# Attention pairs ahead of soft MoE slots: the V products of a pair moved into one block, one pair later

## Chip, cores, metric

The kernel runs on one core of one Trainium2 chip. The metric is the device time of one execution in microseconds (us). Smaller is better.

## The reference, cut to what matters

```python
# attention: q, k, v of 8 batches x 12 heads x 448 tokens x 64
scores = q @ k.T / 8
m = scores.max(-1)
e = exp(scores - m)
attn = e / (e.sum(-1) + exp(-m) + 1e-9)
x = attn @ v                       # then heads side by side: 3584 x 768
# soft MoE: phi 768 x 32, 8 experts of 4 slots, F = 1024
logits = x @ phi
d = softmax of logits over all tokens (per slot)
slot_input = d.T @ x
slot_out[e] = relu(slot_input[e] @ w1[e]) @ w2[e]
c = softmax of logits over the slots (per token)
out = c @ slot_out
```

## The kernel before

Two heads make a pair, and there are 48 pairs (`NPAIR`), six to a batch (`PB`) and three to a group (`NP`). One core does them one after the other; the order on every engine is the order in which the Python code emits the instructions (`manual_schedule`), so the loop over `s` at L646 is the schedule, written out by hand.

What is done to pair `n`:

- `T(n)` (L236): TensorE turns q and k, 28 transposes in quarter tiles (64x64) of the array, into one PSUM tile `ps_t`. From pair 8 on it comes from the pool `psA`, which has three buffers. VectorE (L257), or for every third pair ScalarE (L255), copies it to a tile of `qk_t`, of which there are `NQK` = 7.
- `A1(n, i, hl)` (L287) and `A(n, 3)` (L278): scores with queries on the partitions, each in a tile `ps_a` of the same pool `psA`; VectorE takes the row maxima from it (L292, L285). That makes seven `ps_a` and one `ps_t` for a pair, all through the three buffers in turn.
- `W2(g)`, `W3(g)` (L295, L305): for a group, the maxima are turned to a row by TensorE, three chunks in the full array (L299) and the half chunk in two quarter tiles (L302), and ScalarE copies them and takes the exponentials of the maxima.
- `Bk(n, 3)` (L318) and, inside `AB`, `scores` and `less` (L357, L361): scores with keys on the partitions, less the maxima, in tiles `ps_b` of the pool `psB` (four buffers); ScalarE takes the exponentials (L364, L343) into tiles `e2_t` (`NE` = 5, two heads in each) and `e1_t`.
- `AB(s, i)` (L347) puts six matmuls of half the array's rows together: one `A1` of a pair further ahead, two `scores`, two `less`, and the other `A1`. Two matmuls in different halves of the rows run at once.
- `AV(n, i, qs)` (L385): products of the exponentials with V, added up in the one tile `ps_av` of `psV`. For `qs` = `range(3)` each is in the full array; for `qs` = `[3]` it is in half the array's columns (128x64). 24 of the first kind and 8 of the second make a pair.
- `N1(n)` (L403) copies the result out of PSUM on ScalarE, `N2(n)` (L412) divides: two small VectorE instructions (L418, L419) and three on GpSimd (L423 to L428). `PX(n)` (L442) turns the result on TensorE, and ScalarE copies it (L455).
- `P(b)` (L462) is the soft MoE part of batch `b`, in six steps that the dictionary `post` (L590) lays into the pairs of the next batch.

A pair's round has two halves (`y`). In the first stand `AB(s,0)`, `AB(s,1)`, the V products `AV(s-1, 2..3)`, the eight half column ones of pair `s-1`, and `N1(s-1)`. In the second stand `AB(s,2)`, `Bk(s,3)`, `T(s+6)`, `W2`/`W3` in every third round, `AV(s, 0..1)`, a step of `post`, `PX(s-2)` and `N2(s-1)`. GpSimd's queue also issues the loads (`load`, `load_half`, `narrow`, L702 to L727) and places V (`V`, L376).

After the pairs, the expert matmuls (`hidden`, `turn`, `slots`) and the output follow; they depend on the last batch's maxima, and the output's writes end the kernel.

Of the kernel before, what the change touches and what calls it, by code (L numbers as in the profile page):

```python
# [24 lines left out]
HG = 6  # L25
NP = 3
W65 = 65
VS = 66


@with_exitstack
def kernel(
# [10 lines left out]
    nc = tc.nc  # L43
# [32 lines left out]

    NQK, NE, VPN, NATV = 7, 5, HG * 4 * VS, HG * 4 * D
    sizes = [("nq0", 2 * NP * S), ("nq1", 2 * NP * S), ("nv", NATV), ("qk6", 2 * S), ("wm1", 512),  # L80
             ("qk0", 2 * S), ("qk1", 2 * S), ("qk2", 2 * S), ("wm0", 512), ("qk3", 2 * S), ("vp0", VPN),
             ("qk4", 2 * S), ("x0", 4 * DD), ("qk5", 2 * S), ("e2", NE * 2 * S), ("e1", S), ("vp1", VPN),
             ("xT", KC * 512), ("x1", 4 * DD)]
# [5 lines left out]
    part = lambda nm, o, z: R[:, at_[nm] + o:at_[nm] + o + z]  # L89
    qk_t = [part(f"qk{i}", 0, 2 * S).rearrange("p (a s) -> p a s", a=2) for i in range(NQK)]  # L90
    e2_t = [part("e2", i * 2 * S, 2 * S).rearrange("p (h s) -> p h s", h=2) for i in range(NE)]
    e1_t = part("e1", 0, S)
    vp = [part(f"vp{i}", 0, VPN).rearrange("p (h i d) -> p h i d", h=HG, i=4) for i in range(2)]
    wm = [part(f"wm{i}", 0, 512).rearrange("p (i c) -> p i c", i=4) for i in range(2)]
    xb = [part(f"x{i}", 0, 4 * DD).rearrange("p (i d) -> p i d", i=4) for i in range(2)]
# [47 lines left out]
    with ExitStack() as at:  # L143
# [81 lines left out]

        ec, mT, eT, av, us = {}, {}, {}, {}, {}
        qkT = {}
        st = {"e2": 0}


        def kcol(hl, tok):
# [30 lines left out]
        mg = lambda n: 0 if n == 0 else n // NP + 1  # L262

        def top(n, i, hl=0):
            c = 64 * hl + n % NP
            return wm[mg(n) % 2][:, i, c:c + 1]

        def A(n, i):
            t = qkT[n]
# [25 lines left out]
        def W2(g):  # L295
            w = wm[g % 2]
            ps = pb_("ps_m")
            for i in range(3):
                nc.tensor.matmul(ps[:, i * 128:(i + 1) * 128], w[:, i, :], ident, start=True, stop=True)  # L299
            for hl in range(2):  # L300
                r = slice(64 - 64 * hl, 128 - 64 * hl)
                nc.tensor.matmul(ps[64 * hl:64 * hl + 64, 384:448], w[r, 3, 0:64], ident[r, r], start=True, stop=True)  # L302
            st["ps_m"] = ps

        def W3(g):  # L305
            t = psm.tile([128, S], BF16, tag="mT", name="mT")
            nc.scalar.copy(t, st["ps_m"][:, 0:S])
            mT[g] = t
            e = psm.tile([128, NP, 7], F32, tag="ec", name="ec", bufs=3)
            w = wm[g % 2]  # L310
            nc.scalar.activation(e[:, :, 0:6].rearrange("p l (i h) -> p i l h", i=3),
                                 w[:, 0:3, :].rearrange("p i (h c) -> p i c h", h=2)[:, :, 0:NP, :],
                                 AF.Exp, scale=-scale)
            nc.scalar.activation(e[:, :, 6], w[:, 3, 0:NP], AF.Exp, scale=-scale)
            ec[g] = e


        def Bk(n, i, c=0):  # L318

            g, pl = divmod(n, NP)  # L320
            t = qkT[n]
            rs = [slice(0, 64), slice(64, 128)]
            if i < 3:
                pss = [pb_("ps_b") for _ in range(2)]
                outs = [p[:, 0:S] for p in pss]
                cols = slice(i * 128, (i + 1) * 128)
                e = e2_t[st["e2"] % NE]
                st["e2"] += 1
                es = [e[:, hl, :] for hl in range(2)]
            else:  # L330
                pss = [pb_("ps_b")]
                outs = [pss[0][r, 0:S] for r in rs]
                cols = slice(384, 448)
                es = [e1_t]
            m = cols.stop - cols.start
            for hl in range(2):
                nc.tensor.matmul(outs[hl], t[rs[hl], 1, cols], t[rs[hl], 0, :], start=True, stop=False)  # L337
            As(c)
            for hl in range(2):
                nc.tensor.matmul(outs[hl], sel[rs[hl], pl:pl + 1].to_broadcast([64, m]), mT[mg(n)][rs[hl], :],  # L340
                                 start=False, stop=True)
            for p, e in zip(pss, es):
                nc.scalar.activation(e, p[:, 0:S], AF.Exp, scale=scale)  # L343
            for hl in range(2):
                eT[n, i, hl] = es[hl % len(es)]

        def AB(n, i):  # L347


            t, pl = qkT[n], n % NP  # L350
            run = runs.pop(0) if runs else None
            cols = slice(i * 128, (i + 1) * 128)
            e = e2_t[st["e2"] % NE]
            st["e2"] += 1
            rs, ps = [slice(0, 64), slice(64, 128)], {}

            def scores(hl):  # L357
                ps[hl] = pb_("ps_b")
                nc.tensor.matmul(ps[hl][:, 0:S], t[rs[hl], 1, cols], t[rs[hl], 0, :], start=True, stop=False)  # L359

            def less(hl):  # L361
                nc.tensor.matmul(ps[hl][:, 0:S], sel[rs[hl], pl:pl + 1].to_broadcast([64, 128]), mT[mg(n)][rs[hl], :],  # L362
                                 start=False, stop=True)
                nc.scalar.activation(e[:, hl, :], ps[hl][:, 0:S], AF.Exp, scale=scale)  # L364
                eT[n, i, hl] = e[:, hl, :]

            if run:
                A1(*run, 0)
            scores(1)
            scores(0)  # L370
            less(1)
            less(0)
            if run:
                A1(*run, 1)
# [87 lines left out]
        def P(b):  # L462
# [62 lines left out]

            def corr():
                if b:
                    t = psm.tile([128, NS], F32, tag="corr", name="corr")
                    nc.scalar.activation(t, v["z"][:, 8, :], AF.Exp)
                    v["corr"] = t  # L530

# [14 lines left out]
            def c_turn():  # L546
                ps = pa([128, 128], BF16, "ps_ct")
                nc.tensor.transpose(ps, flat(v["cd"][:, 0:4, :]), ident)
                nc.vector.tensor_copy(cT[:, b // 2, :, b % 2, :], ps.rearrange("p (h j) -> p h j", h=2))
                r = crec[:, b, :]  # L550
                nc.vector.reduce_sum(r, v["cd"][:, 0:4, :], axis=AX.X)
                nc.vector.tensor_scalar(r, r, 1e-9, None, op0=ALU.add)
                nc.vector.reciprocal(r, r)

            def s_add():
                if b:
# [4 lines left out]
            def s_last():  # L561

                h = KC // 2
                s_mm(0, h)
                nc.vector.tensor_add(siT[:, 0:h, :], acc[:, 0:h, :], v["ps_s"])
                s_mm(h, KC + 1)
                ps = v["ps_s"]
                nc.vector.tensor_add(siT[:, h:KC, :], acc[:, h:KC, :], ps[:, 0:KC - h, :])
                t = psm.tile([128, NS], F32, tag="corr", name="srow")
                nc.vector.scalar_tensor_tensor(t, acc[:, KC, :], 1e-9, ps[:, KC - h, :], op0=ALU.add, op1=ALU.add)  # L570

                nc.vector.tensor_mul(t, t, fold)
                nc.vector.reduce_sum(hrec, t, axis=AX.X)
                nc.vector.reciprocal(hrec, hrec)
# [12 lines left out]

        post = {}  # L590
        for b in range(B - 1):
            for z, f in enumerate(P(b)):
                post[2 * (PB * b + PB + 2) + z + (z > 2) + (z > 4) if b < B - 2 else 2 * (PB * b + PB + 2) - 1 + z] = f

        ub = ubuf.rearrange("p n c -> p (n c)").bitcast(BF16)
        take = lambda z, n: ub[:, z:z + n]
# [38 lines left out]
        for z in range(2):  # L635
# [4 lines left out]
        half_at = {s: i for i, s in enumerate((1, 4, 7, 10, 13, 16, 22, 25, 28, 31, 34))}  # L640

        narrow_at = {18: 4, 19: 5, 20: 6, 35: 7}
        part_at = {38: ((11, 0, 3),), 41: ((11, 3, 7),), 42: ((11, 7, 8),)}
        col_at = {42: ((0, 0, 8),), 43: ((1, 0, 2),), 44: ((1, 2, 6),), 45: ((1, 6, 8), (2, 0, 4), (3, 0, 6)),
                  46: ((2, 4, 8),), 47: ((3, 6, 8),)}
        for s in range(NPAIR):  # L646
            for y in range(2):
                hs = 2 * s + y
                early, last_ = int(hs < 5), int(hs < 3)
                if early:  # L650
# [13 lines left out]
                if hs < 5:  # L664
                    T(hs + 3)
                if y == 0:
                    if 0 <= s - 1:
                        for i in (2, 3):
                            AV(s - 1, i, range(3))
                else:  # L670
                    if 2 <= s < NPAIR - 6:
                        T(s + 6)
                    g = (s + 1) // 3
                    if (s + 1) % 3 == 0 and g < NG:
                        W2(g + 1)
                        W3(g + 1)
                    if s < NPAIR:
# [6 lines left out]
                if y and 0 <= s - 2 < NPAIR - 2 and s - 2 != n6:  # L684
                    PX(s - 2)
                if hs == 2 * n6 + 4:
                    PX(n6)
# [11 lines left out]
                if hs == 1:  # L699
                    W2(1)  # L700
                    W3(1)
            g = (s + 10) // 3  # L702
            if s == 1 or s % 3 == 2:
                g = 3 if s == 1 else g
                if (s == 1 or g > 3) and g < NG:
                    load(g, "q")
                    load(g, "k")
            g = (s + 9) // 3
            if s % 3 == 0 and g - 2 < NG:
                V(g - 2)  # L710
# [185 lines left out]
```

## Time and profile before

| what | value |
|---|---|
| runs | 307.33, 308.73, 309.12 us; median 308.73 us |
| profiled execution | 309.52 us, its span (first to last instruction) 307.7 us |
| busy in the span | TensorE 279.3 us (91%), VectorE 257.1 (84%), ScalarE 250.9 (82%), GpSimd 184.9 (60%) |
| chain that ended last | TensorE 69%, VectorE 14%, ScalarE 8%, issue 3% |
| granted TensorE clock | 1.00 up to 275 us, 0.58 in the last 32.7 us |
| pairs in their regular order | about 40 us to 240 us, 30.1 to 31.3 us for six pairs |
| maxima, L292 | 254 instructions, 140.0 us busy, 615 ns each |
| exponentials, L364 | 272 instructions, 131.0 us busy, 573 ns each |
| V products, L397 | 1536 instructions, 64.6 us busy |

Busy times are sums over the rows of an engine, with overlap counted once. A row of TensorE lasts from the start of a matmul until its last result is out (353 ns for 448 columns), though the next one begins much earlier; how fast TensorE goes is read from start to start. Rows of VectorE and ScalarE overlap a little too: a maximum has a row of 615 ns, but a run of six lasts less than six times that.

### The profile page before, as it was taken

Reading aid. Unit: us, or ns where it says so; the run is one execution under the profiler, and the core shown is the slowest. Engines: PE = TensorE matmul, PEld = TensorE weight load, DVE = VectorE, ACT = ScalarE, POOL = GpSimd, SP = SyncE. Lnnn points to the kernel's source line nnn. Section 1 sums busy time; section 2 is a strip of 40 time slices with the busy share of each in tenths; the row PEclk is TensorE's granted clock in tenths of the full one; section 3 lists DMA queues with packets and bytes.
Section 4 is the critical chain, followed back from the end, with each engine's and each line's share of the span. In section 5 each row is a group of like instructions: output and inputs, shape, how many; then the busy total and the mean of one; then the engine's idle time right before and its main releaser. Section 6 shows DMA issues by size and latency. Waiting matters only on the chain.

```text
span 307.7 us, 12173 instructions
## 1 busy us (share of the span) xinstructions
PE 279.3 (91%) x5097; PEld 159.8 (52%) x5097; DVE 257.1 (84%) x604; ACT 250.9 (82%) x551; POOL 184.9 (60%) x336
## 2 busy tenths in 40 slices
PE   7999999999999999999999999999999999995900
PEld 2444656566565656555656565656564555441100
DVE  7899999999999999989999999999999676446910
ACT  3477999999999999989999999999999995345800
POOL 9681986968586869866877677686747662000000
PEclk9999999999999999999999999999999999997555
DMA  8999999999999999999999999999845899909995
GB/s 134 134 158 184 139 210 202 195 197 165 191 161 198 164 200 148 202 184 151 120 202 134 197 179 204 151 200 205 141 56 88 124 137 224 362 32 341 433 426 229
DMA packets 49384, 57.69 MB, mean 188 GB/s; under 512 B 2865, under 2 KB 41521, under 8 KB 48945
## 3 DMA queue, kind: packets, MB, share of 16 engines
q0 software_dynamic: 45280, 42.29, 89.6%
q1 hardware_dynamic: 4048, 14.62, 12.1%
q8 instruction: 40, 0.66, 0.8%
q14 instruction: 16, 0.12, 0.1%
HBM read 88.18 MB, written 14.16 MB: 333 GB/s over the span
## 4 chain that ended last, share of the span: by engine, by line
PE 69%; DVE 14%; ACT 8%; issue 3%; POOL 1%; DVEq 0%; POOLq 0%
PE ps_av L397 15%; PE ps_a L291 9%; PE ps_t L251 7%; PE ps_b L359 7%; PE ps_b L362 6%; DVE R L292 6%; PE ps_b L337 4%; PE ps_b L340 2%; ACT R L343 2%; DVE R L277 2%; PE ps_x L449 2%; PE ps_o L802 2%; PE ps_a L274 2%; PE ps_so L773 2%; ACT R L255 2%
## 5 line engine op out<-in xcount | busy, mean ns | idle before, releaser
L292 DVE TENSOR_REDUCE R<-ps_a 128x1 bf16<-128x448 f32 x254 | 140.0, 615 | 6.4 <-PE ps_a L291 5.5
L364 ACT ACTIVATE R<-ps_b 128x448 bf16<-128x448 f32 x272 | 131.0, 573 | 0.5 <-PE ps_b L362 0.2
L291 PE MATMUL ps_a<-R 64*128 64x448 bf16 x254 | 83.2, 353 | 1.5 <-DVE R L292 1.5
L359 PE MATMUL ps_b<-R 64*128 64x448 bf16 x272 | 74.5, 353 | 1.1
L362 PE MATMUL ps_b<-mT,sel 64*128 64x448 bf16 x272 | 71.3, 350 | 0.0
L423 POOL TENSOR_TENSOR R<-ubuf,rec 128x384 bf16<-128x384 f32 x44 | 36.2, 823 | 55.1 <-DVE rec L419 33.7
L397 PEld LDWEIGHTS <-R 128*128 128x128 bf16 (+1 forms) x1536 | 50.0, 100 | 30.8 <-issue 26.1
L397 PE MATMUL ps_av<-R 128*128 128x65 bf16 (+1 forms) x1536 | 64.6, 196 | 0.0
L343 ACT ACTIVATE R<-ps_b 128x448 bf16<-128x448 f32 x64 | 35.9, 579 | 2.7 <-PE ps_b L340 2.6
L251 PEld LDWEIGHTS <-R 64*64 64x64 bf16 x1344 | 30.0, 112 | 12.6 <-issue 4.9
L455 ACT CAST R<-ps_x 128x512 bf16<-128x512 f32 x47 | 28.1, 599 | 6.9 <-PE ps_x L449 6.4
L251 PE MATMUL ps_t<-ident,R 64*64 64x64 bf16 x1344 | 31.2, 196 | 0.6
L285 DVE TENSOR_REDUCE R<-ps_a 128x1 bf16<-128x448 f32 x48 | 29.6, 617 | 0.6 <-PE ps_a L283 0.6
L362 PEld LDWEIGHTS <-sel 64*128 64x128 bf16 x272 | 21.8, 94 | 15.1 <-issue 5.5
L291 PEld LDWEIGHTS <-R 64*128 64x128 bf16 x254 | 23.8, 94 | 11.1 <-issue 1.1
L409 ACT COPY ubuf<-ps_av 128x455 f32<-128x455 f32 x44 | 25.1, 570 | 2.4 <-POOL R L428 2.2
L255 ACT COPY R<-ps_t 128x896 bf16<-128x896 bf16 x20 | 18.4, 922 | 6.0 <-PE ps_t L251 5.6
L337 PE MATMUL ps_b<-R 64*64 64x448 bf16 (+1 forms) x112 | 21.9, 375 | 0.0
L277 DVE TENSOR_REDUCE R<-ps_a 128x1 bf16<-128x448 f32 x34 | 18.9, 618 | 2.1 <-PE ps_a L274 2.0
L340 PE MATMUL ps_b<-mT,sel 64*64 64x448 bf16 (+1 forms) x112 | 20.5, 353 | 0.0
L428 POOL TENSOR_TENSOR R<-ubuf,rec 128x128 bf16<-128x128 f32 x44 | 17.5, 398 | 3.7
L359 PEld LDWEIGHTS <-R 64*128 64x128 bf16 x272 | 17.2, 94 | 4.7 <-issue 0.3
(137 smaller groups left out, 439.7 us busy)
## 6 DMA issues: line engine op xcount, KB each, us to landing
W<-in_moe_w_dram POOLq DMA_DIRECT2D x22, 768.0 KB, 10.2
R<-in_v_dram POOLq DMA_DIRECT2D x32, 192.0 KB, 4.9
out_dram<-W SPq DMA_DIRECT2D x2, 2688.0 KB, 11.8
R<-in_q_dram POOLq DMA_DIRECT2D x14, 336.0 KB, 7.9
R<-in_k_dram POOLq DMA_DIRECT2D x14, 336.0 KB, 9.0
wd<-in_moe_w_dram POOLq DMA_DIRECT2D x8, 384.0 KB, 10.7
R<-wd SPq DMA_DIRECT2D x8, 384.0 KB, 8.2
R<-in_moe_w_dram POOLq DMA_DIRECT2D x2, 768.0 KB, 8.1
```

The source lines that it names most:

```text
L251: nc.tensor.transpose(ps[r, a, c:c + 64], src[r, pl, tok * D:(tok + 1) * D], ident[r, r])
L285: nc.vector.reduce_max(top(n, i), ps[:, 0:S], axis=AX.X)
L291: nc.tensor.matmul(ps[:, 0:S], t[r, 0, i * 128:(i + 1) * 128], t[r, 1, :], start=True, stop=True)
L292: nc.vector.reduce_max(top(n, i, hl), ps[:, 0:S], axis=AX.X)
L337: nc.tensor.matmul(outs[hl], t[rs[hl], 1, cols], t[rs[hl], 0, :], start=True, stop=False)
L343: nc.scalar.activation(e, p[:, 0:S], AF.Exp, scale=scale)
L359: nc.tensor.matmul(ps[hl][:, 0:S], t[rs[hl], 1, cols], t[rs[hl], 0, :], start=True, stop=False)
L362: nc.tensor.matmul(ps[hl][:, 0:S], sel[rs[hl], pl:pl + 1].to_broadcast([64, 128]), mT[mg(n)][rs[hl], :], start=False, stop=True)
L364: nc.scalar.activation(e[:, hl, :], ps[hl][:, 0:S], AF.Exp, scale=scale)
L397: nc.tensor.matmul(o, eT[n, i, hl][:, qc], vp[g % 2][:, 2 * pl + hl, i, 0:W65], start=(i == 0 and u == 0 and hl == 0), stop=(i == 3), skip ...
L423: eng.tensor_mul(x[:, 0:3, c:c + 128].rearrange("p i (h d) -> p i h d", h=2), u[:, 0:6, 0:D].rearrange("p (i h) d -> p i h d", h=2), rec[: ...
L455: nc.scalar.copy(xT[:, pb, :], pss[0])
```

## The change

- From pair 3 (`S0`) to pair 40 (`S1` - 1) a round is written by a new function `pair(s)`. The three `AB` stand one after the other, then `Bk(s,3)`, `T(s+5)`, in every third round `W2`/`W3`, a step of `post`, `PX(s-3)`, and then all 32 V products of pair `s-1` in one block. `N1(s-1)` stands at the end, and `N2(s-2)` between the second and the third `AB`. The first three pairs and the last seven keep the old order, with a round in which it goes over at each end.
- For this there are six tiles of exponentials for two heads (`NE` and one more, `e5`), two for the half chunk (`e1_t`), and six tiles of turned q and k in place of seven. `T` runs five pairs ahead and not six.
- The half chunk's maxima lie elsewhere in `wm`, so that `W2` turns them by two matmuls over 128 and 120 columns in the full array's shape, not by two of 64x64.
- The steps of `post` go one to a round; `1e-9` and the reciprocal of `crec` are done once for all batches at the end, not per batch; the tile `corr` has one buffer.
- The loads of q and k stand at the end of rounds 0, 3, 6, ... and not 2, 5, 8, ...; the parts of one expert's weights (`part_at`) are loaded at 39 and 42, and not at 38, 41 and 42.

```diff
+HALF = 392
...
-    NQK, NE, VPN, NATV = 7, 5, HG * 4 * VS, HG * 4 * D
+    NQK, NE, VPN, NATV = 6, 5, HG * 4 * VS, HG * 4 * D
...
-    e1_t = part("e1", 0, S)
+    e2_t.append(part("e5", 0, 2 * S).rearrange("p (h s) -> p h s", h=2))
+    e1_t = [part("e1", 0, S), keep.tile([128, S], BF16, name="e1b")]
...
+        def next_e2(n):
+            if n == S1 and NE in free:
+                free.remove(NE)
+            free.append(free.pop(0))
+            return e2_t[free[-1]]
...
-            for hl in range(2):
-                r = slice(64 - 64 * hl, 128 - 64 * hl)
-                nc.tensor.matmul(ps[64 * hl:64 * hl + 64, 384:448], w[r, 3, 0:64], ident[r, r], start=True, stop=True)
+            f = w.rearrange("p i c -> p (i c)")
+            nc.tensor.matmul(ps[:, 384:448], f[:, HALF - 64:HALF + 64], ident[:, 0:64], start=True, stop=False)
+            nc.tensor.matmul(ps[0:512 - HALF, 384:448], f[:, HALF:512], ident[:, 64:128], start=False, stop=True)
...
-                nc.vector.reduce_sum(r, v["cd"][:, 0:4, :], axis=AX.X)
-                nc.vector.tensor_scalar(r, r, 1e-9, None, op0=ALU.add)
-                nc.vector.reciprocal(r, r)
+                nc.vector.reduce_sum(crec[:, b, :], v["cd"][:, 0:4, :], axis=AX.X)
+                if b == B - 1:
+                    nc.vector.tensor_scalar(crec, crec, 1e-9, None, op0=ALU.add)
+                    nc.vector.reciprocal(crec, crec)
...
+        S0, S1 = 3, NPAIR - 7
...
-                post[2 * (PB * b + PB + 2) + z + (z > 2) + (z > 4) if b < B - 2 else 2 * (PB * b + PB + 2) - 1 + z] = f
+                if b == B - 2:
+                    post[2 * (PB * b + PB + 2) - 1 + z] = f
+                elif PB * b + PB + 3 + z < S1:
+                    post[2 * (PB * b + PB + 3 + z) + 1] = f
+                else:
+                    post[max(post) + 1] = f
...
-        part_at = {38: ((11, 0, 3),), 41: ((11, 3, 7),), 42: ((11, 7, 8),)}
+        part_at = {39: ((11, 0, 3),), 42: ((11, 3, 8),)}
...
+        def pair(s):
+            AB(s, 0)
+            AB(s, 1)
+            if s > S0:
+                N2(s - 2)
+            AB(s, 2)
+            Bk(s, 3, 1)
+            T(s + 5)
+            if (s + 1) % 3 == 0:
+                W2((s + 1) // 3 + 1)
+                W3((s + 1) // 3 + 1)
+            if 2 * s + 1 in post:
+                post[2 * s + 1]()
+            PX(s - 3)
+            for i in range(4):
+                AV(s - 1, i, range(3))
+            for i in range(4):
+                AV(s - 1, i, [3])
+            N1(s - 1)
+
         for s in range(NPAIR):
-            for y in range(2):
+            if S0 <= s < S1:
+                pair(s)
+            for y in range(0 if S0 <= s < S1 else 2):
...
-            g = (s + 10) // 3
-            if s == 1 or s % 3 == 2:
-                g = 3 if s == 1 else g
-                if (s == 1 or g > 3) and g < NG:
-                    load(g, "q")
-                    load(g, "k")
+            g = 3 if s == 1 else (s + 9) // 3
+            if (s == 1 or s > 2 and s % 3 == 0) and g < NG:
+                load(g, "q")
+                load(g, "k")
```

More of the change, by code (lines that the diff above doesn't have):

```diff
@@ L75 @@
     halfm = const.tile([128, 2], F32, name="halfm")
-    NQK, NE, VPN, NATV = 7, 5, HG * 4 * VS, HG * 4 * D
-    sizes = [("nq0", 2 * NP * S), ("nq1", 2 * NP * S), ("nv", NATV), ("qk6", 2 * S), ("wm1", 512),
+    NQK, NE, VPN, NATV = 6, 5, HG * 4 * VS, HG * 4 * D
+    sizes = [("nq0", 2 * NP * S), ("nq1", 2 * NP * S), ("nv", NATV), ("e5", 2 * S), ("wm1", 512),
              ("qk0", 2 * S), ("qk1", 2 * S), ("qk2", 2 * S), ("wm0", 512), ("qk3", 2 * S), ("vp0", VPN),
@@ L227 @@
         qkT = {}
-        st = {"e2": 0}
+        st = {"e1": 0}
+        free = list(range(NE + 1))
+        def next_e2(n):
[3 more added lines that the diff above has]
+            return e2_t[free[-1]]
         def kcol(hl, tok):
@@ L264, in top @@
         def top(n, i, hl=0):
-            c = 64 * hl + n % NP
-            return wm[mg(n) % 2][:, i, c:c + 1]
+            c = n % NP + (HALF if i == 3 else i * 128 + 64 * hl)
+            return wm[mg(n) % 2].rearrange("p i c -> p (i c)")[:, c:c + 1]
         def A(n, i):
@@ L313, in W3 @@
                                  AF.Exp, scale=-scale)
-            nc.scalar.activation(e[:, :, 6], w[:, 3, 0:NP], AF.Exp, scale=-scale)
+            nc.scalar.activation(e[:, :, 6], w[:, 3, HALF - 384:HALF - 384 + NP], AF.Exp, scale=-scale)
             ec[g] = e
@@ L326, in Bk @@
                 cols = slice(i * 128, (i + 1) * 128)
-                e = e2_t[st["e2"] % NE]
-                st["e2"] += 1
+                e = next_e2(n)
                 es = [e[:, hl, :] for hl in range(2)]
@@ L333, in Bk @@
                 cols = slice(384, 448)
-                es = [e1_t]
+                es = [e1_t[st["e1"] % 2]]
+                st["e1"] += 1
             m = cols.stop - cols.start
@@ L352, in AB @@
             cols = slice(i * 128, (i + 1) * 128)
-            e = e2_t[st["e2"] % NE]
-            st["e2"] += 1
+            e = next_e2(n)
             rs, ps = [slice(0, 64), slice(64, 128)], {}
@@ L527, in corr @@
                 if b:
-                    t = psm.tile([128, NS], F32, tag="corr", name="corr")
+                    t = psm.tile([128, NS], F32, tag="corr", bufs=1, name="corr")
                     nc.scalar.activation(t, v["z"][:, 8, :], AF.Exp)
@@ L549, in c_turn @@
                 nc.vector.tensor_copy(cT[:, b // 2, :, b % 2, :], ps.rearrange("p (h j) -> p h j", h=2))
-                r = crec[:, b, :]
-                nc.vector.reduce_sum(r, v["cd"][:, 0:4, :], axis=AX.X)
-                nc.vector.tensor_scalar(r, r, 1e-9, None, op0=ALU.add)
-                nc.vector.reciprocal(r, r)
+                nc.vector.reduce_sum(crec[:, b, :], v["cd"][:, 0:4, :], axis=AX.X)
+                if b == B - 1:
+                    nc.vector.tensor_scalar(crec, crec, 1e-9, None, op0=ALU.add)
+                    nc.vector.reciprocal(crec, crec)
             def s_add():
@@ L568, in s_last @@
                 nc.vector.tensor_add(siT[:, h:KC, :], acc[:, h:KC, :], ps[:, 0:KC - h, :])
-                t = psm.tile([128, NS], F32, tag="corr", name="srow")
+                t = psm.tile([128, NS], F32, tag="corr", bufs=1, name="srow")
                 nc.vector.scalar_tensor_tensor(t, acc[:, KC, :], 1e-9, ps[:, KC - h, :], op0=ALU.add, op1=ALU.add)
@@ L666 @@
                 if y == 0:
+                    if s == S1:
+                        N2(s - 2)
+                        PX(s - 3)
                     if 0 <= s - 1:
-                        for i in (2, 3):
+                        for i in range(0 if s == S1 else 2, 4):
                             AV(s - 1, i, range(3))
                 else:
-                    if 2 <= s < NPAIR - 6:
-                        T(s + 6)
+                    if S1 <= s < NPAIR - 5:
+                        T(s + 5)
                     g = (s + 1) // 3
@@ L676 @@
                         W3(g + 1)
-                    if s < NPAIR:
+                    if s != S0 - 1:
                         for i in (0, 1):
@@ L683 @@
                     nc.vector.reduce_max(fold, ident.rearrange("p (i s) -> p s i", i=4), axis=AX.X)
-                if y and 0 <= s - 2 < NPAIR - 2 and s - 2 != n6:
+                if y and S1 <= s < NPAIR and s - 2 != n6:
                     PX(s - 2)
```

## The prediction

> **What bounds the kernel now.** I read the busy times by stage first, then the waits, then the order of time on TensorE and on VectorE. In the stages, three engines are nearly full at once:
>
> ```profile
> 101.40:131.70 30.30, 29.83 (x604) 18.43 (x602) 28.75 (x69) 28.71 (x67) 24.04 (x43) 1.00 1.14 178
> ```
>
> The columns are stretch and length, then busy us of TensorE, weight loads, VectorE, ScalarE and GpSimd, then the granted clock. Six pairs take 30.3 us, 5.05 us each. VectorE and ScalarE are busy 4.79 us of a round, so if VectorE never waited, a round could lose 0.26 us at most. The waits from 71.3 to 223.1 us, about thirty rounds, say that it hardly waits, and that TensorE hardly waits for it:
>
> ```profile
> DVE R L292 <- PE ps_a L291: 3.4, 10, 0.3
> ...
> PE ps_a L291 <- DVE R L292: 1.2, 5, 0.2
> ```
>
> In the same stretch no row shows the transposes (L251) waiting for VectorE at all. The balance holds because V products and other work stand between groups of score matmuls in portions that the three `ps_a` buffers cover. In the order of time on TensorE (start, us, line; a row ends when its last result is out, so progress is read from start to start):
>
> ```profile
> 128.37 0.36 PE L291 MATMUL ps_a<-R 64*128 64x448 bf16 x1
> ...
> 131.58 0.63 PE L251 MATMUL ps_t<-ident,R 64*64 64x64 bf16 x28
> 132.14 0.54 PE L397 MATMUL ps_av<-R 128*128 128x65 bf16 x12
> 132.51 0.60 PE L543 MATMUL ps_s<-cd,R 128*128 128x32 bf16 x18
> ...
> 134.01 0.38 PE L449 MATMUL ps_x<-ident,R 128*128 128x128 bf16 x4
> 134.32 0.36 PE L291 MATMUL ps_a<-R 64*128 64x448 bf16 x1
> ...
> 134.72 0.54 PE L291 MATMUL ps_a<-R 64*128 64x448 bf16 x2
> 134.91 0.54 PE L359 MATMUL ps_b<-R 64*128 64x448 bf16 x2
> ...
> 135.44 0.35 PE L291 MATMUL ps_a<-R 64*128 64x448 bf16 x1
> 135.72 0.79 PE L397 MATMUL ps_av<-R 128*128 128x65 bf16 x20
> 136.44 0.36 PE L291 MATMUL ps_a<-R 64*128 64x448 bf16 x1
> ```
>
> and on VectorE:
>
> ```profile
> 118.07 0.15 DVE L418 SCALAR_TENSOR_TENSOR rec<-ubuf,ec 128x7 f32<-128x7 f32 x1
> 118.26 0.20 DVE L419 RECIPROCAL rec<-rec 128x7 f32<-128x7 f32 x1
> 118.38 2.17 DVE L292 TENSOR_REDUCE R<-ps_a 128x1 bf16<-128x448 f32 x4
> ...
> 128.77 3.28 DVE L292 TENSOR_REDUCE R<-ps_a 128x1 bf16<-128x448 f32 x6 [0.34 <-PE ps_a L291]
> 131.97 0.62 DVE L285 TENSOR_REDUCE R<-ps_a 128x1 bf16<-128x448 f32 x1
> ```
>
> From these come all the prices. Matmuls of 448 columns in different row halves run two at a time, 0.19 us a couple (134.72 to 134.91). Where the shape of the tile changes, the step is 0.28 us (135.44 to 135.72), so a change costs 0.09. `T` with its change of shape takes 0.56 (131.58 to 132.14), twelve full V products 0.37 (132.14 to 132.51), twelve and the eight half column ones with two changes 0.72 (135.72 to 136.44), `PX` 0.31 with a change, 0.22 without. The first maximum after an idle VectorE starts 0.40 after its matmul (128.37 to 128.77). Maxima follow one another at 0.53 ((3.28 - 0.62) / 5), and the two instructions of `N2` take 0.31 (118.07 to 118.38).
>
> **The new round, step by step.** A round has eight tiles of `psA`: `ps_a` 1 to 6 from the three `AB`, 7 from `Bk`, and `ps_t`. With three buffers taken in turn, `ps_t` gets the buffer of tile 5, so `T` starts only when the fifth maximum is done. No work of TensorE stands between the `AB` any more, so it runs ahead until the buffers are full, and VectorE sets the pace up to there. Counted from the first matmul of `AB(s,0)`:
>
> - first maximum starts: 0.40
> - four maxima at 0.53: 2.12
> - `N2(s-2)` on VectorE, now between the fourth and the fifth: 0.31
> - the fifth maximum to its end: 0.62
> - from there to `T`: 0.05 (an estimate; a matmul that waits for a maximum starts about that long after its end). `T` at 3.50.
> - `T` and the change of shape: 0.56
> - `PX(s-3)`: 0.22
> - 32 V products: 0.37 + 0.72 = 1.09, the change back to `AB` within it.
>
> The plain round is 3.50 + 1.87 = 5.37 us. When `T` starts, VectorE has two maxima left (1.06) and, in two rounds of three, the copy of `ps_t` (0.61): 1.67 us. Until its next maximum TensorE needs 1.87 + 0.40 = 2.27, so VectorE idles 0.6 us, and 1.2 where ScalarE takes the copy. `T` is the added wait: behind it in TensorE's queue are `W2`, `post`, `PX`, all V products and the next `AB`, so VectorE waits for its maxima and ScalarE for its exponentials.
>
> What else stands behind `T` lengthens the round in full, since VectorE has no work to hide it. Per six rounds: 24 matmuls of `l_mm`, 0.60, and 28 of `s_mm`, 0.70, both at 25 ns (18 to 0.45 in the rows at 132.51); `l_turn` 0.14; the matmuls of `s_max` and `c_turn` 0.06 each; two `W2` at 0.22 (three at 55 ns as in `PX`, two at 29 ns as the V products). Together 2.0, or 0.33 a round. The mean round is 5.70 us against 5.05: +0.65. There are 38 of them: +24.7 us.
>
> **The savings, counted within this.** The shape changes fall from six a round to four, and in `W2` by two per three rounds: (0.18 + 0.06) x 38 = 9 us of TensorE's time. They are already in the 1.87 and the 0.22, and what TensorE gains it waits for at `T`.
>
> The Trainium skill says (TensorEngine Tiling (Array Packing), Key Properties) that a change of tiling mode drains TensorE; this trace agrees, with 0.09 us for one. By that rule alone the new order would be 9 us faster, which is the first rival. The skill also gives about 81 ns for each of a stream of weight load and 128 column matmul (TensorE: Matmul & The Clock Gate, Back-to-back issue gap); by that the four of `PX` would be 0.1 us longer than the 0.22 here, some 4 us over all rounds, and the rows at 134.01 and 134.32 decide for 0.22.
>
> **Edits that I cost at nothing.** The twelve V products that leave pair 2's round come into pair 3's, and those of pair 40 into 41: no sum. Two tiles for the half chunk and six for the exponentials: `AV(s-1)` ends before `AB(s+1)` on TensorE's own queue, so no new wait. `T` five pairs ahead: its pair's first maximum is in the third `AB` of the next round, some 1.87 + 1.6 us after `T` starts, and the copy is done 1.2 us after that start (1.5 to 2 on ScalarE); if it were late, `AB` would wait by what is missing. `N2(s-2)` and `PX(s-3)`: GpSimd has at least a round for its 1.5 us (L423 to L428); without that cover `PX` would wait up to 1.5. The loads of q and k now pass `V` and the load of v in GpSimd's queue, two issues of 0.8 us: V is needed four rounds later, q and k after about 9 us are needed four rounds later too; a late one would cost those 1.6 us. They wait for `T` of the same round, and GpSimd stands meanwhile, with its 24.0 us of 34. The later `part_at` loads have the expert matmuls' start some 20 us behind them; 8 us to landing, 0 to 2 us if that fails. The fewer `crec` instructions (0.35 us, six times) lie on VectorE, which idles there.
>
> **Bounds.** No row shows `T` waiting for a maximum, `W2` in its new shape, or the whole block. `N2`'s pair may hide to 0.22 or cost 0.42 as a dependent pair; the block may be 1.75 (V products at a steady 29 ns) or 1.95; the extras 0.27 to 0.40. The round is then 5.5 to 5.9, +17 to +32 us. I take the middle values, since each is the row of that very instruction.
>
> The sum against the profiled execution: 309.52 + 24.7 = 334.2; that execution was 0.8 above the median, so against the median 308.73 + 24.7 = 333.4.
>
> **Rivals.**
>
> - TensorE is the bound, and the changes of shape decide. Then the round falls by 0.24 us towards VectorE's 4.79: about 299.5. For it: TensorE is busy 29.8 of 30.3. Against it: that is rows with their latency in them. It decides when the work from `T` to the next `AB` falls below what VectorE holds, 1.67 - 0.40 = 1.27 us; it is 1.87. Chance 0.04.
> - The extra work of `post` and `W2` falls into waits of TensorE, and of the idle 0.6 a part is made good by VectorE starting the next `AB` with both buffers free: +0.3 a round, 320. Against it: the queue is in order, and these steps stand behind `T`. Chance 0.06.
> - ScalarE falls behind as well: `PX`'s copy (0.6), `N1` (0.57) and, in two rounds of three, the copy of `ps_t` (0.92) or of the maxima (0.53 and two small ones) come at the end of the block, and the exponentials of the next `AB` start late, so that TensorE also waits for `psB`. 0.3 in two rounds of three is 0.2 x 38 = 7.6 more: 341. For it: ScalarE is as full as VectorE now. Against it: an exponential every 0.44 is faster than a maximum. Chance 0.07.
> - The clock falls, as in the last 32.7 us (0.58) where TensorE mostly waits. At half, the block and its extras take 2.2 more: +84 us, 417. Against it: the longest wait in the new round is at `T`, under 1 us, and the clock is 1.00 all through the pairs. Chance 0.02.
>
> **How the numbers follow.** My forecast, a bubble of VectorE in every round, has 0.81. The range, 326 to 341, takes in its costs' bounds on both sides but their outermost ends, and the third rival; outside are the others. Half a per cent, 1.5 us, is about what a measurement of this kernel can tell from no change. Faster is the first rival, 0.04; no change 0.01, for its weaker form; the rest slower.
>
> **What would show it.** In the profile of after: six pairs in 34 us, not 30.3, with VectorE's busy time about the same (28.4), so 83% and not 95%; the idle time of L292's successor before `PE ps_a` at 0.6 us or more a round, above 20 us in all; the transposes waiting for a maximum, some 0.5 to 0.9 us a round; V products in one run of 32 of about 1.1 us. It is wrong if VectorE stays above 90% in these stages, or if the transposes don't wait.

## The result: 8.2% slower, and the profile after

| | before | changed |
|---|---|---|
| median | 308.71 us | 335.19 us |
| range of the runs | 307.33 to 309.12 | 333.63 to 335.50 |
| profiled execution, its span | 309.52, 307.7 us | 335.5, 333.7 us |

The ratio is 1.082, with a 95% interval from 1.078 to 1.087. The forecast was 333.4 us, with a range from 326 to 341. Ratios here and below are of the runs in the faster of two states alone, which leaves out three of the twelve runs of experiment 7 and none of the others.

The chain that ended last has changed hands. Before, TensorE had 69% of it and VectorE 14%. Now (the profile's chain by engine, then the longest lines of it):

```profile
PE 48%; DVE 40%; ACT 3%; issue 2%; DMA 1%; POOL 1%; DVEq 0%; POOLq 0%
DVE R L301 31%; PE ps_av L405 13%; PE ps_t L260 8%; PE ps_a L300 5%; PE ps_x L457 3%; DVE rec L427 2%; DVE R L286 2%; PE ps_so L810 2%; PE ps_o L839 2%; PE ps_h L794 2%; PE ps_s L551 2%; PE ps_l L483 2%; PE ps_a L283 1%; DMA R<-in_q_dram 1%; PE ps_warm L183 1%
```

The maxima (now L301) are 31% of it, and the V products (L405) and the transposes (L260) follow. Six pairs, in the busy times by stage, with the columns as in the prediction:

```profile
101.40:135.70 34.30, 30.69 (x599) 19.16 (x595) 28.51 (x67) 29.13 (x67) 23.90 (x42) 1.00 1.01 160
```

Six rounds take 34.3 us, not 30.3. VectorE does the same work in them, 28.5 us against 28.8, and so is busy 83% of the time and not 95%. The clock is 1.00. The waits from 71.3 to 223.1 us, as before:

```profile
DVE R L301 <- PE ps_a L300: 17.9, 18, 1.2
...
PE ps_t L260 <- DVE R L301: 10.8, 25, 0.8
...
DVE R L301 <- PE ps_b L367: 6.1, 9, 0.8
...
PE ps_a L300 <- DVE R L301: 5.0, 27, 0.2
```

The columns are total us, times, and longest. VectorE's waits before its first maximum were 3.4 us in this stretch and are 17.9 + 6.1 us, in 27 rounds. (The second is the same wait; there the profile names the matmul that stood beside the `ps_a` one.) The transposes' wait for a maximum had no row before, and is 10.8 us in 25 rounds. Both are there at once: each engine waits for the other, at different places of a round.

One plain round on TensorE, from 152.00 to 157.34 us:

```profile
152.00 0.36 PE L300 MATMUL ps_a<-R 64*128 64x448 bf16 x1
...
155.47 0.63 PE L260 MATMUL ps_t<-ident,R 64*64 64x64 bf16 x28 [0.42 <-DVE R L301]
156.03 0.40 PE L457 MATMUL ps_x<-ident,R 128*128 128x128 bf16 x4
156.27 0.71 PE L405 MATMUL ps_av<-R 128*128 128x65 bf16 x18
...
157.34 0.36 PE L300 MATMUL ps_a<-R 64*128 64x448 bf16 x1
```

and the same on VectorE:

```profile
152.40 2.22 DVE L301 TENSOR_REDUCE R<-ps_a 128x1 bf16<-128x448 f32 x4 [0.61 <-PE ps_b L367]
154.53 0.16 DVE L426 SCALAR_TENSOR_TENSOR rec<-ubuf,ec 128x7 f32<-128x7 f32 x1
154.73 0.20 DVE L427 RECIPROCAL rec<-rec 128x7 f32<-128x7 f32 x1
154.84 1.11 DVE L301 TENSOR_REDUCE R<-ps_a 128x1 bf16<-128x448 f32 x2
155.87 0.62 DVE L294 TENSOR_REDUCE R<-ps_a 128x1 bf16<-128x448 f32 x1
156.40 0.62 DVE L266 COPY R<-ps_t 128x896 bf16<-128x896 bf16 x1
157.74 2.22 DVE L301 TENSOR_REDUCE R<-ps_a 128x1 bf16<-128x448 f32 x4 [0.72 <-PE ps_a L300]
```

Read the two together: four maxima, `N2`'s pair, the fifth maximum, which ends at 155.42, and 0.05 us later the transposes. While TensorE then does the transposes, `PX` and the V products up to 157.34, VectorE finishes what it holds at 157.02 and idles 0.72 us.

The wait of the transposes itself is not new, though it had no row. In the kernel before, the six maxima that begin at 128.77 (the row stands in the prediction) have the fifth one's end at about 128.77 + 4 x 0.53 + 0.62 = 131.51, and the transposes start at 131.58. No idle time shows, because the row of the matmuls ahead of them is not over yet:

```profile
131.33 0.35 PE L340 MATMUL ps_b<-mT,sel 64*64 64x448 bf16 x2
```

In the traces of both kernels the transposes start 0.05 us after the end of the fifth maximum, in each of the 38 rounds that the change rewrites: 3.46 us after the begin of `AB(s,0)` before and 3.49 us now, on average. What has grown is the stretch from there to the next `AB`, with the V products in it: 1.55 us before and 2.17 now. That is 0.62 of the 0.66 us by which a round is longer.

### The profile page after: what moved, and what is told of

Read it like the earlier page. It is cut to its first block, busy times and chain, and to the rows that moved or that the text cites. A ratio compares the mean times of both kernels' runs of the same rounds, so it can differ in the third digit from the quotient of the medians.

```text
span 333.7 us, 12323 instructions
## 1 busy us (share of the span) xinstructions
PE 283.2 (85%) x5097; PEld 163.9 (49%) x5097; DVE 255.7 (77%) x590; ACT 253.0 (76%) x551; POOL 184.3 (55%) x335
## 4 chain that ended last, share of the span: by engine, by line
PE 48%; DVE 40%; ACT 3%; issue 2%; DMA 1%; POOL 1%; DVEq 0%; POOLq 0%
DVE R L301 31%; PE ps_av L405 13%; PE ps_t L260 8%; PE ps_a L300 5%; PE ps_x L457 3%; DVE rec L427 2%; DVE R L286 2%; PE ps_so L810 2%; PE ps_o L839 2%; PE ps_h L794 2%; PE ps_s L551 2%; PE ps_l L483 2%; PE ps_a L283 1%; DMA R<-in_q_dram 1%; PE ps_warm L183 1%
## 5 line engine op out<-in xcount | busy, mean ns | idle before, releaser
L301 DVE TENSOR_REDUCE R<-ps_a 128x1 bf16<-128x448 f32 x254 | 141.0, 612 | 35.8 <-PE ps_a L300 26.9
L372 ACT ACTIVATE R<-ps_b 128x448 bf16<-128x448 f32 x272 | 124.7, 565 | 0.7 <-PE ps_b L370 0.5
L300 PE MATMUL ps_a<-R 64*128 64x448 bf16 x254 | 81.9, 350 | 7.4 <-DVE R L301 7.0
L431 POOL TENSOR_TENSOR R<-ubuf,rec 128x384 bf16<-128x384 f32 x44 | 36.2, 822 | 74.9 <-DVE rec L427 46.5
L367 PE MATMUL ps_b<-R 64*128 64x448 bf16 x272 | 72.7, 352 | 0.6 <-ACT R L463 0.3
L370 PE MATMUL ps_b<-mT,sel 64*128 64x448 bf16 x272 | 70.5, 349 | 0.6 <-ACT mT L316 0.5
L405 PE MATMUL ps_av<-R 128*128 128x65 bf16 (+1 forms) x1344 | 52.9, 195 | 0.0
L405 PEld LDWEIGHTS <-R 128*128 128x128 bf16 (+1 forms) x1344 | 44.2, 100 | 7.4 <-issue 4.5
L260 PE MATMUL ps_t<-ident,R 64*64 64x64 bf16 x1344 | 30.8, 195 | 16.6 <-DVE R L301 16.1
L260 PEld LDWEIGHTS <-R 64*64 64x64 bf16 x1344 | 29.5, 111 | 29.9 <-issue 29.0
L417 ACT COPY ubuf<-ps_av 128x455 f32<-128x455 f32 x44 | 23.7, 540 | 11.4 <-PE ps_av L405 8.3
L370 PEld LDWEIGHTS <-sel 64*128 64x128 bf16 x272 | 24.4, 94 | 12.5 <-issue 3.6
L352 ACT ACTIVATE R<-ps_b 128x448 bf16<-128x448 f32 x40 | 22.0, 574 | 3.5 <-PE ps_b L349 3.5
L349 PE MATMUL ps_b<-mT,sel 64*64 64x448 bf16 (+1 forms) x112 | 21.7, 373 | 0.0
```

Source lines behind the costliest of these rows:

```text
L260: nc.tensor.transpose(ps[r, a, c:c + 64], src[r, pl, tok * D:(tok + 1) * D], ident[r, r])
L300: nc.tensor.matmul(ps[:, 0:S], t[r, 0, i * 128:(i + 1) * 128], t[r, 1, :], start=True, stop=True)
L301: nc.vector.reduce_max(top(n, i, hl), ps[:, 0:S], axis=AX.X)
L405: nc.tensor.matmul(o, eT[n, i, hl][:, qc], vp[g % 2][:, 2 * pl + hl, i, 0:W65], start=(i == 0 and u == 0 and hl == 0), stop=(i == 3), skip ...
L417: (nc.scalar.copy if on_pool(n) else nc.vector.tensor_copy)(u, src)
L431: eng.tensor_mul(x[:, 0:3, c:c + 128].rearrange("p i (h d) -> p i h d", h=2), u[:, 0:6, 0:D].rearrange("p (i h) d -> p i h d", h=2), rec[: ...
```

## The experiments

Theory 1 is that of the prediction: with three buffers in turn the transposes wait for the fifth maximum, and the block behind them is longer than what VectorE holds by then. Rival 2: a round is as long as TensorE's own work in the new order, and the buffers do not matter. Rival 3: ScalarE's exponentials come late and hold TensorE. "A round" below is the mean of the 38 changed rounds, from one `AB(s,0)` to the next on TensorE in the trace; it is 5.01 us before and 5.67 in the changed kernel. Where two parts of it are named, they are the time from `AB(s,0)` to the start of the transposes and the time from there to the next `AB`, on average: 3.49 and 2.17 us in the changed kernel.

**1. Four buffers for the maxima, three for the exponentials** (in the changed kernel)

```diff
-        psA = pool("psA", 3, space=PSUM)
-        psB = pool("psB", 4, space=PSUM)
+        psA = pool("psA", 4, space=PSUM)
+        psB = pool("psB", 3, space=PSUM)
```

> The changed kernel with four buffers for the maxima's scores (psA) and three for the exponentials' (psB). Theory 1 (three psA buffers hold the transposes until the fifth maximum, and VectorE starves in the block): the transposes wait only for the fourth maximum, VectorE enters the block with one maximum more, its idle time before the first maximum of a round falls by about 0.5 us, and the round falls from 5.67 to 4.9 to 5.2 us: 307 to 318 us. Rival 2 (the round is as long as TensorE's own work, the block included): the buffers don't matter, 334 to 336 us. Rival 3 (ScalarE's exponentials come late and hold TensorE): one psB buffer fewer makes it worse, over 337 us.

Measured: 323.71 us, ratio to before 1.047 (1.042 to 1.051), a round of 5.37. That is 11.5 us less than the changed kernel, and misses the range of theory 1 by 6 us. The waits from 100 to 234 us:

```profile
DVE R L301 <- PE ps_a L300: 15.6, 25, 0.9
PE ps_b L367 <- ACT R L372: 14.9, 50, 0.3
```

TensorE has no row left in which the transposes wait for a maximum, and by the trace they start before the fifth one has ended (by 0.22 us in most rounds), as theory 1 says. In its place stands a new wait, twice a round and 0.6 us in all: the scores for the exponentials wait for ScalarE, which still holds one of the three buffers. So rival 3 is no cause of the change's loss, but ScalarE holds TensorE as soon as one of its buffers is taken away. VectorE's wait before a round's first maximum is 0.62 us a round, 0.88 in the changed kernel: half of the 0.5 expected. The run moves one buffer from the one pool to the other, and wins more at the transposes than it loses at the new wait.

**2. `N2` behind the transposes on VectorE**

```diff
             AB(s, 1)
-            if s > S0:
-                N2(s - 2)
             AB(s, 2)
             Bk(s, 3, 1)
             T(s + 5)
+            if s > S0:
+                N2(s - 2)
```

> The changed kernel with the two VectorE instructions of N2 behind the transposes' copy instead of between the fourth and fifth maximum; TensorE's order is the same. Theory 1: they leave the stretch that ends in the transposes, where they take 0.31 us, and go into VectorE's idle time: 38 x 0.31 = 12 us less, 322 to 325 us. Rival 2: TensorE's work is the same, 334 to 336 us. Rival 3: 334 to 336 us.

Measured: 325.59 us, ratio 1.052 (1.048 to 1.056), a round of 5.42. TensorE's instructions are the same and in the same order; two instructions of VectorE, of 0.36 us by their rows, moved out of the stretch before the fifth maximum, and the time fell by 9.6 us. Rival 2 can't have that. It is a little less than the 12 us that were summed up (0.25 a round and not 0.31). The waits have only one row of 0.2 us left in which the transposes wait for a maximum, but that is the overlap of TensorE's rows again. One round:

```profile
152.02 3.28 DVE L301 TENSOR_REDUCE R<-ps_a 128x1 bf16<-128x448 f32 x6 [0.41 <-PE ps_a L300]
```

```profile
154.83 0.63 PE L260 MATMUL ps_t<-ident,R 64*64 64x64 bf16 x28
```

The fifth maximum ends at about 152.02 + 4 x 0.53 + 0.62 = 154.76, and the transposes follow. In all 38 rounds they start 0.05 us after it, as in the changed kernel. The two parts of the round are 3.25 and 2.18 us: the whole gain lies ahead of the transposes, and the fifth maximum still sets their start. So the missing 0.06 us is the price of the pair, which was put too high: in the changed kernel the maximum right behind the pair lasts 0.58 us, and here, behind another maximum, it lasts 0.61.

**3 and 4. The V products between the second and the third `AB`**: twelve of them, and then the whole block with `N1`

```diff
# 3
             AB(s, 1)
             if s > S0:
                 N2(s - 2)
+            for i in (0, 1):
+                AV(s - 1, i, range(3))
             AB(s, 2)
...
-            for i in range(4):
+            for i in (2, 3):
                 AV(s - 1, i, range(3))
# 4
+            for i in range(4):
+                AV(s - 1, i, range(3))
+            for i in range(4):
+                AV(s - 1, i, [3])
+            N1(s - 1)
             AB(s, 2)
...
-            for i in range(4):
-                AV(s - 1, i, range(3))
-            for i in range(4):
-                AV(s - 1, i, [3])
-            N1(s - 1)
```

> The changed kernel with twelve of the 32 V products (chunks 0 and 1) between the second and the third AB, the other twenty at the end; a pair later still. Theory 1: the block behind the transposes is 0.37 us shorter, and the twelve hide under VectorE's maxima: 38 x 0.37 = 14 us less, 319 to 323 us. Rival 2: TensorE's work is the same and two changes of tile shape (0.18 us) more, so 335 to 342 us. Rival 3: the exponentials of the third AB come later, 335 us or more.

> The changed kernel with the whole block of 32 V products and N1 between the second and the third AB; the rest of the round as it was. Theory 1: behind the transposes only 0.56 + 0.22 + 0.09 us are left, a plain round would be 4.4 us by that chain, so VectorE's own 4.75 us decide; TensorE's 1.2 us of block are covered by the three buffers' 1.6 us and N2's 0.31. Round 4.8 to 4.95 us, 302 to 308 us, a little below the kernel before. Rival 2: 335 us or more. Rival 3: N1 stands before the third AB's exponentials, 325 to 335 us.

Measured: 321.77 us, ratio 1.040 (1.036 to 1.043), a round of 5.31, for the twelve; 309.23 us, ratio 1.000 (0.997 to 1.002), a round of 4.98, for the block. The twelve V products give 13.4 us for the 14 expected, with two changes of shape more on TensorE; the part behind the transposes fell from 2.17 to 1.81 us, and the one ahead of them stayed at 3.50. The block in the middle takes the whole loss back, with all other parts of the change still in place. It is the same block of the same pair, with the same tiles; only its place in the round differs, and that of `N1` behind it. So it is not the V products in one block that cost, but where the block stands. Experiment 4, TensorE and then VectorE:

```profile
140.31 0.63 PE L260 MATMUL ps_t<-ident,R 64*64 64x64 bf16 x28
...
141.21 0.36 PE L300 MATMUL ps_a<-R 64*128 64x448 bf16 x1
...
142.83 1.15 PE L405 MATMUL ps_av<-R 128*128 128x65 bf16 x32
143.91 0.36 PE L300 MATMUL ps_a<-R 64*128 64x448 bf16 x1
```

```profile
141.24 0.61 DVE L266 COPY R<-ps_t 128x896 bf16<-128x896 bf16 x1
141.77 2.21 DVE L301 TENSOR_REDUCE R<-ps_a 128x1 bf16<-128x448 f32 x4
```

What stood in one piece of 1.87 us now stands in two, and VectorE has about enough in hand for each, with the 0.40 us from the next scores to their maximum. From the transposes to the next scores it is 0.90 us, and VectorE is at work until 141.77, 1.46 us after the transposes' start. The block takes 1.08 us, and when it begins VectorE has two of its four maxima and the pair of `N2` before it, which is 1.06 + 0.31. VectorE's wait for the maxima in experiment 4, from 100 to 234 us:

```profile
DVE R L301 <- PE ps_a L300: 2.1, 9, 0.3
```

Its time lies 1.2 us above the expected range. Two things were not in that sum: the time from `AB(41,0)` to the end is 85.0 us here, 82.7 before (experiments 9 and 10 have 83.7 and 83.2, so how much of the 2.3 us is the going over to the old order stays open), and a stall on VectorE that is told at the end.

**5. The tile of the transposes from the exponentials' buffers** (in the changed kernel)

```diff
-            tp, tg = (psB, "b") if n < 8 else (psA, "a")
+            tp, tg = (psB, "b")
```

> The changed kernel with the tile of the turned q and k taken from the exponentials' four buffers (psB) and not from the maxima's three. Theory 1: the transposes no longer wait for the fifth maximum; Bk's scores for the maxima still wait for the fourth (0.40 + 3 x 0.53 + 0.62 + 0.05 = 2.66), then 0.45 us of Bk stand before the transposes, so these start at 3.0 to 3.1 and not at 3.47, and the next AB finds more free buffers: 38 x 0.4 to 0.6, 312 to 320 us. Rival 2: 334 to 336 us. Rival 3 (ScalarE late): the transposes then wait for an exponential and the time stays over 328 us.

Measured: 314.40 us, ratio 1.018 (1.014 to 1.021), a round of 5.12. One line gives back 20.8 of the 26.5 us, with all of the block still behind the transposes. Theory 1's range holds it; the two parts of the round are 2.91 and 2.21 us, the first a little less than the 3.0 to 3.1 expected. Here the transposes start before the fifth maximum has ended, by 0.53 us in most rounds, and wait for none, while the scores for the maxima still do, 0.18 us a round as in the changed kernel.

**9 and 10. More work for TensorE, in two places**: `PX`'s four matmuls done twice behind the transposes; and the two score matmuls for the maxima in the third `AB` done twice, ahead of the transposes

```diff
# 9, in PX
+                for _ in range(2 if 0 <= n < S1 - 3 else 1):
-                nc.tensor.matmul(pss[i // 2 if two else 0][:, o:o + 128], x[:, i, c], ident if i < 3 else ident2,
-                                 start=True, stop=True)
+                    nc.tensor.matmul(pss[i // 2 if two else 0][:, o:o + 128], x[:, i, c], ident if i < 3 else ident2,
+                                     start=True, stop=True)
# 10, in A1, with more = 2 for chunk 2 of the pairs from S0 to S1 - 1
+            for _ in range(more):
-            nc.tensor.matmul(ps[:, 0:S], t[r, 0, i * 128:(i + 1) * 128], t[r, 1, :], start=True, stop=True)
+                nc.tensor.matmul(ps[:, 0:S], t[r, 0, i * 128:(i + 1) * 128], t[r, 1, :], start=True, stop=True)
```

> The changed kernel with PX's four matmuls done twice in the 38 rounds (the second time over the first, so the values stay): 0.22 us more of TensorE's work, behind the transposes. Theory 1: nothing hides it, 38 x 0.22 = 8.4 us more than the changed kernel, 342 to 345 us. Rival 2: the same, 342 to 345 us; it differs in the next run.

> The changed kernel with the two score matmuls for the maxima of one AB done twice in some 35 rounds (again over the first): two matmuls of 448 columns more, 0.2 to 0.4 us of TensorE's work, in the stretch that VectorE paces. Theory 1: TensorE waits there anyway for the fifth maximum, so it costs nothing, 334 to 336.5 us. Rival 2 (the round is TensorE's own work): 35 x 0.2 to 0.4 = 7 to 13 us more, 342 to 348 us.

Measured: 343.16 us, ratio to before 1.108 (1.104 to 1.112), a round of 5.90; and 333.54 us, ratio 1.079 (1.074 to 1.084), a round of 5.67. Behind the transposes 0.22 us of matmuls cost 0.23 us a round: the two parts are 3.50 and 2.40 us. Ahead of them, two matmuls of 448 columns cost nothing (3.49 and 2.17 us; the time is even 0.5 us below the expected range). This separates the theories most plainly: a round has a stretch, behind the transposes, where TensorE's time has its full price and one where it has none. In the second, TensorE only waits less (the transposes' wait from 100 to 234 us, first the changed kernel, then experiment 10):

```profile
PE ps_t L260 <- DVE R L301: 9.2, 22, 0.4
```

```profile
PE ps_t L260 <- DVE R L302: 7.2, 24, 0.3
```

**6, 7 and 8. Parts on the kernel before.** In 6 it has the wide turn of the half chunk alone, in 7 the transposes' tile from psB alone (the line of experiment 5), and in 8 both, with `crec`'s reciprocals once at the end. The order of the V products is the old one in all three.

```diff
# 6 and 8, in W2; the columns in top() and W3 as in the change
-            for hl in range(2):
-                r = slice(64 - 64 * hl, 128 - 64 * hl)
-                nc.tensor.matmul(ps[64 * hl:64 * hl + 64, 384:448], w[r, 3, 0:64], ident[r, r], start=True, stop=True)
+            f = w.rearrange("p i c -> p (i c)")
+            nc.tensor.matmul(ps[:, 384:448], f[:, HALF - 64:HALF + 64], ident[:, 0:64], start=True, stop=False)
+            nc.tensor.matmul(ps[0:512 - HALF, 384:448], f[:, HALF:512], ident[:, 64:128], start=False, stop=True)
```

> The kernel before with one part of the change alone: the half chunk of the maxima turned by two wide ranges in the full array's shape, 0.2 us of TensorE's time and two changes of shape less in each third round. Theory 1 (in the order before, too, VectorE and its buffers set the pace, and TensorE's savings are waited away): 0 to 2 us less than before, 306.8 to 309 us. Rival 2 (TensorE's work sets the round): 16 x 0.2 = 3.2 us less, 305 to 306 us.

> The kernel before with one new edit alone: the tile of the turned q and k from psB. Theory 1: the maxima's three buffers then hold maxima only, the next AB's first scores need not wait for the copy of the turned q and k, and VectorE's waits (3.4 us in thirty rounds) shrink: 1 to 4 us less than before. Rival 2: the same as before. Rival 3: psB with nine tiles a round holds TensorE back, slower than before.

> The kernel before with three small parts together: the wide turn of the half chunk, the tile of the turned q and k from psB, and the reciprocals of crec once at the end (0.35 us of VectorE six times). The old order of the V products stays. Theory 1: each part takes something off VectorE's round or its waits: 3 to 7 us less than before, 302 to 306 us, faster than both kernels. Rival 2: only the wide turn counts, 305 to 306 us. Rival 3: slower than before.

Measured: 306.39 us, ratio 0.992 (0.989 to 0.995); 308.16 us, ratio 0.995 (0.992 to 0.998); 303.56 us, ratio 0.981 (0.977 to 0.985). The three ratios are 2.6, 1.6 and 5.8 us. Experiment 6 lies between the two expectations, 0.4 us below the range of theory 1 and 0.4 above that of rival 2. Its interval, 1.7 to 3.5 us, holds the full saving of 3.2, so in the old order this work of TensorE counts for the most part. The traces say why: `W2` stands behind the transposes, and they wait for the fifth maximum in the old order too. A round is 4.95 us for 5.01, and all of the difference lies behind the transposes (1.49 us for 1.55). So VectorE does not set the pace alone there, and neither does TensorE. Experiment 7 is too small an effect to choose between theory 1 and rival 2 (0.9 us by the medians of all runs); only rival 3 is out. Experiment 8 is faster than both kernels. Its VectorE is nearly full, 29.2 us in 30.3 (29.1 on average over four such stretches):

```profile
101.40:131.70 30.30, 30.04 (x625) 19.19 (x623) 29.22 (x69) 29.44 (x68) 25.06 (x45) 1.00 1.17 184
```

So the wide turn of the half chunk is good by itself, and the change as a whole hides it under the loss from the block's place. The reciprocals of `crec` were not run alone.

## Why the prediction was right

**The round.** It was summed up to 5.37 us for a plain round, and 152.00 to 157.34 is 5.34. The steps came out one by one: the first maximum 0.40 us after its matmul (152.00 to 152.40), `N2`'s pair 0.31 (154.53 to 154.84), the transposes at 3.47 (predicted 3.50), from there to the next `AB` 1.87 (predicted 1.87), VectorE idle 0.61 and 0.72 (predicted 0.6). The 0.03 at the transposes is the fifth maximum, 0.58 long and not 0.62; by experiment 2 the pair so costs 0.25 in all, and the term of 0.31 was a little too large. The mean of the 38 rounds is 5.67; the prediction had 5.70.

**The sum.** The 38 rounds take 215.4 us, and 190.4 before: 24.95 us more, for 24.7. The remaining 1.05 us of the 26.0 us between the two spans are the edges, which the prediction had at nothing: the first changed round begins 1.3 us sooner (twelve V products of pair 2 and `T(8)` now come after its begin), at 33.2 us, and the rest from `AB(41,0)` on is 2.4 us longer, 85.1 us. Other executions differ by more than this: in the experiments on the changed kernel, which leave the order there as it is, the first begins at 30.4 to 33.3 us and the second takes 83.2 to 86.3. So whether the zero was wrong by 1 us stays open.

**The signs it named.** Six pairs in 34 us, VectorE at 83%, its waits above 20 us and the block in one run of 32 are all there. The transposes' wait by the row is 0.4 us a round, a little below the 0.5 to 0.9 named; the wait in that row begins when the engine runs dry, which is 0.35 us after the last matmul's start, and the sum did not use it.

**The rivals.** That the changes of tile shape would decide was wrong: they cost time only where they stand behind the transposes. Experiment 3 has two more of them ahead of the transposes and still gave 13.4 of the 14 us; experiment 6 has two fewer behind them, in each third round, and gave most of their price. The Trainium skill says (TensorEngine Tiling (Array Packing), Key Properties) that a change of mode drains TensorE; in this kernel such a price is paid only where another engine waits for what comes behind it. That the extra work of `post` and `W2` falls into waits is refuted too: the mean round is 0.33 us longer than the plain one, which is the full sum of that work, and in experiment 9 other work at the same place had its full price. That ScalarE falls behind did not happen with four buffers; experiment 1 shows that it would with three. The clock stayed at 1.00 in the 38 rounds. In the profiled execution of the changed kernel it was 0.50 to 0.78 from 8 to 17 us, ahead of them; in that of experiment 10 it was 1.00 there, and the 38 rounds took the same time, 215.3 us.

**What the prediction did not see**: that the transposes waited for the fifth maximum in the old order as well. It read from the missing row that TensorE hardly waits for VectorE, took VectorE's 4.79 us of 5.05 for the whole bound, and called the wait of the transposes added. By the traces the wait was there in every round, and the change put 0.62 us more work behind it. This did not touch the forecast, since the new round is built from its own steps and the old one is a measured time.

## What to carry to other kernels

Before putting work together to save changes of mode, list for each engine what it has in hand when the block begins: here two maxima and a copy, 1.7 us, against 1.9 us of work and 0.4 more until the next maximum can begin. The same V products cost 26 us at the end of the round and nothing between two groups of matmuls, so the place counts and not the block. A missing wait row does not mean that nothing waits: compare the start of an instruction with the end of what it needs. And where tiles of two kinds share a ring of buffers, count back through the ring whose reader must be done: one line that gave the transposes another ring won back 21 of those 26 us.

## What the runs showed of the hardware

A short VectorE instruction can be held by GpSimd. In experiment 4 `N2`'s first instruction (L426: two small inputs in SBUF) takes 0.62 us in some rounds, where its usual row is 0.16. First VectorE, then GpSimd:

```profile
143.89 0.62 DVE L426 SCALAR_TENSOR_TENSOR rec<-ubuf,ec 128x7 f32<-128x7 f32 x1
```

```profile
143.83 0.66 POOL L387 COPY R<-R 128x576 bf16<-128x576 bf16 x1
```

It begins within the copy of V on GpSimd and ends 0.02 us after it (144.51 and 144.49), and so in four rounds with 0.62 to 0.65 us; five more have 0.30 to 0.39. Over the usual row that is 2.8 us in all. In experiment 2 another VectorE instruction with two SBUF inputs, L523, takes 0.82 to 1.09 us in five rounds, where its usual row is 0.19, and ends 0.05 us behind a GpSimd instruction (L431). The Trainium skill (SBUF — State Buffer, Who interferes with whom) says that the two engines share one pair of ports as an exclusive lock, and that a VectorE instruction with two SBUF inputs contends with a GpSimd one that reads SBUF. These rows agree. The maxima, which read PSUM, kept their 0.53 us beside the same copies.
